# Batches two to four of a linear-attention and mixture-of-experts kernel: query features stream past stationary key sums, and denominators come out on the other 64 partitions

## The chip, the core and the metric

One core of a Trainium2 chip runs the whole program. The metric is the device time of one execution in microseconds (us); lower is better. The engines named below are PE (TensorE matmul; PEld is its weight load), DVE (VectorE), ACT (ScalarE), POOL (GpSimd) and SP (SyncE, which issues most DMAs). Each engine works through its own instruction list in the order in which the program writes it.

## The reference

Random-feature attention over 4 batches, 8 heads, 576 positions and 64 dimensions, with 128 features, and then a dense mixture of 4 experts on the 2304 tokens.

```python
def phi(x):                       # x scaled by 64 ** -0.25
    h = einsum('bhsd,md->bhsm', x, omega) - sum(x * x, -1, keepdims=True) / 2
    return exp(h - max(h, -1, keepdims=True)) / sqrt(m)
kv  = einsum('bhsm,bhsd->bhmd', k_p, v)
z   = sum(k_p, axis=2)
num = einsum('bhsm,bhmd->bhsd', q_p, kv)
den = einsum('bhsm,bhm->bhs', q_p, z)[..., None] + 1e-06
x   = (num / den), heads side by side: [2304, 512]
p   = domain_probs / (sum(domain_probs, -1) + 1e-09)
out = sum over e of p[:, e:e+1] * (relu(x @ w1[e]) @ w2[e])   # w1[e] is 512 x 1024
```

## The kernel before

**Experts.** The hidden width of each of the 4 experts is halved, so there are 8 (expert, half) visits for each of 4 token ranges ("u"): 0 to 511, 512 to 1023, 1024 to 1535 and 1536 to 2303. The token-range loop is the outer one. A visit works on blocks of 512 tokens (a few of 256): four *hidden steps* (`hidden`, lines 386 to 394, one of the half's four column groups each, called H0 to H3 below) and then one *output step* for every 128 tokens (`outputs`, lines 402 to 420, called O0 to O3). Numbers are held as two fp32r parts, high and low, and three products (high by high, high by low, low by high) stand for one f32 product. A hidden step on 512 tokens is 12 matmuls of 512 columns; an output step is 12 of 512 columns too. A hidden step ends with `relu` (ACT writes `hh`, then DVE writes `hl`) and, as a rule, one `split_w` (ACT writes a weight's high part, POOL its low part, and SP issues the load of a later weight). An output step ends with an accumulation on DVE (line 418) and one `split_w`. The second argument of the experts' matmuls is read from two rings of 1536 tokens, `x_hi` and `x_lo`.

**Attention.** A `Pair` is two heads of one batch. Batch 0 is done by `Pair`: four pairs in `begin`, before the experts start, and the rest of its queries in `first_rest` during the first visits. Batches 1, 2 and 3 are done by `Halves`, four pairs each, in `later_ticks`: a generator that yields between small parts, called ticks here. For one pair the ticks are, in order:

1. `project` (matmuls of keys and queries with omega into six PSUM banks), maxima of the keys
2. bias and exponentials of keys, first half
3. exponentials of keys, second half
4. the tails (the last 64 positions of both heads)
5. exponentials of queries, first head
6. exponentials of queries, second head; `sum_keys` (matmuls that add up `kv` and the sums `z`); loads of the next pair
7. `turn`: PE transposes of the query features into PSUM, copied to SBUF by DVE as `qt` (first head, and the tails)
8. `turn` of the second head
9. `numerators(0)` (first 256 positions)
10. `numerators(1)` (other 320 positions), `finish(0)`
11. `finish(1)`

In `numerators` the turned query features are the stationary operand and `kvs` (65 columns a head: 64 values and the sum) streams; the result has positions on partitions, so `finish` transposes it again on PE (lines 188 and 190), ACT writes `x_hi` from PSUM and DVE `x_lo`.

**Order.** The program order is written out by hand and kept: each engine executes in the order of emission. `emit` (line 605) walks through the visits; after each step it adds the step's share (1 for a step of 512 columns, 0.5 for a hidden step of 256) to a count and lets the ticks catch up to it. A batch has 48 ticks (4 to load and square the first pair, then 11 for each of 4 pairs), spread evenly over 0.9 of the batch's steps: 1.333 ticks a step for batch 1 (it has only 5 visits, numbers 3 to 7), 0.702 for batch 2 (visits 8 to 15), 0.833 for batch 3 (visits 16 to 23). So in batch 1 two neighbouring ticks now and then stand in one step, with no expert matmul between them; in batches 2 and 3 one or two steps lie between neighbouring ticks.

**PSUM.** All banks come from one pool of 8, handed out in turn by `bank`: the ninth request waits until the first bank has been read for the last time.

## Time and profile before

| | us |
|---|---|
| median of 3 runs | 975.51 (974.34 to 976.88) |
| the profiled execution | 980.6 |
| its span, first to last instruction | 978.2 |
| mean granted TensorE clock, share of full speed | 0.99 |
| PE busy | 957.4 (98%) |
| DVE busy | 369.2 (38%) |
| ACT busy | 342.2 (35%) |
| POOL busy | 371.8 (38%) |

The busy time of PE is made of records whose ends are modelled and overlap, so the pace of matmuls is read from start to start. Times within the trace count from the start of the span.

### The profile page before, as it was taken

Reading aid. Unit: us, or ns where it says so; the run is one execution under the profiler, and the core shown is the slowest. Engines: PE = TensorE matmul, PEld = TensorE weight load, DVE = VectorE, ACT = ScalarE, POOL = GpSimd, SP = SyncE. Lnnn points to the kernel's source line nnn. Section 1 sums busy time; section 2 is a strip of 40 time slices with the busy share of each in tenths; the row PEclk is TensorE's granted clock in tenths of the full one; section 3 lists DMA queues with packets and bytes.
Section 4 is the critical chain, followed back from the end, with each engine's and each line's share of the span. In section 5 each row is a group of like instructions: output and inputs, shape, how many; then the busy total and the mean of one; then the engine's idle time right before and its main releaser. Section 6 shows DMA issues by size and latency. Waiting matters only on the chain.

```text
span 978.2 us, 13669 instructions
## 1 busy us (share of the span) xinstructions
PE 957.4 (98%) x5216; PEld 808.6 (83%) x5216; DVE 369.2 (38%) x760; ACT 342.2 (35%) x806; POOL 371.8 (38%) x312
## 2 busy tenths in 40 slices
PE   6989999999999999999999999999999999999998
PEld 6978888887888888878888888888888888888887
DVE  3434445553334444343333354544311222222222
ACT  3345344433262324334326252434323221322120
POOL 3756543343342234444444344444414422431230
PEclk9799999999999999999999999999999999999999
DMA  6434544232432412423263342422313211221211
GB/s 152 108 107 119 171 126 135 78 111 80 126 89 80 141 48 86 145 69 90 82 202 99 112 135 76 135 78 75 109 63 86 76 34 64 87 65 31 78 33 65
DMA packets 60737, 94.09 MB, mean 96 GB/s; under 512 B 10176, under 2 KB 18560, under 8 KB 60672
## 3 DMA queue, kind: packets, MB, share of 16 engines
q1 hardware_dynamic: 60432, 92.92, 32.4%
q8 instruction: 41, 0.67, 0.3%
q10 hardware_dynamic: 240, 0.30, 0.1%
q14 instruction: 24, 0.20, 0.1%
HBM read 88.48 MB, written 4.72 MB: 95 GB/s over the span
## 4 chain that ended last, share of the span: by engine, by line
PE 94%; ACT 2%; DMA 1%; DVE 1%; POOL 1%; SPq 1%; issue 0%; POOLq 0%; ACTq 0%
PE g L392 14%; PE g L394 14%; PE g L393 14%; PE g L409 13%; PE g L411 13%; PE g L410 13%; PE kv L142 3%; PE nd L166 2%; PE qt_ps L151 2%; PE k_ps L234 1%; PE q_ps L234 1%; PE x_ps L188 1%; PE t_ps L238 1%; DMA k<-in_kT 1%; DMA va<-in_vn 1%; PE k_ps L114 1%
## 5 line engine op out<-in xcount | busy, mean ns | idle before, releaser
L378 POOL TENSOR_TENSOR w1l<-wraw,w1h 128x512 fp32r<-128x512 f32 x128 | 164.5, 1286 | 383.5 <-ACT w1h L375 374.9
L392 PE MATMUL g<-x_hi,w1h 128*128 128x512 f32 (+1 forms) x688 | 252.8, 367 | 0.0
L394 PE MATMUL g<-x_hi,w1l 128*128 128x512 f32 (+1 forms) x688 | 248.0, 360 | 0.0
L393 PE MATMUL g<-x_lo,w1h 128*128 128x512 f32 (+1 forms) x688 | 247.9, 360 | 0.0
L399 DVE SCALAR_TENSOR_TENSOR hl<-g,hh 128x512 fp32r<-128x512 f32 (+1 forms) x172 | 104.1, 605 | 345.4 <-ACT hh L398 345.4
L409 PE MATMUL g<-w2h,hh 128*128 128x512 f32 x576 | 228.4, 397 | 0.2 <-ACT hh L398 0.2
L411 PE MATMUL g<-w2h,hl 128*128 128x512 f32 x576 | 225.5, 391 | 0.0
L410 PE MATMUL g<-w2l,hh 128*128 128x512 f32 x576 | 225.0, 391 | 0.0
L398 ACT ACTIVATE hh<-g 128x512 fp32r<-128x512 f32 (+1 forms) x172 | 91.0, 529 | 375.0 <-PE g L394 374.8
L378 POOL TENSOR_TENSOR w2l<-wraw,w2h 128x512 fp32r<-128x512 f32 x128 | 163.1, 1289 | 144.0 <-ACT w2h L375 143.4
L418 DVE SCALAR_TENSOR_TENSOR acc<-g,pr,acc 128x512 f32<-128x512 f32 x126 | 94.6, 750 | 192.9 <-PE g L411 192.5
L394 PEld LDWEIGHTS g<-x_hi,w1l 128*128 128x128 f32 x688 | 131.0, 190 | 21.0
L392 PEld LDWEIGHTS g<-x_hi,w1h 128*128 128x128 f32 x688 | 131.1, 190 | 20.7 <-issue 0.5
L393 PEld LDWEIGHTS g<-x_lo,w1h 128*128 128x128 f32 x688 | 131.1, 190 | 19.5
L411 PEld LDWEIGHTS g<-w2h,hl 128*128 128x128 f32 x576 | 108.2, 188 | 24.1 <-DVE hl L399 1.1
L409 PEld LDWEIGHTS g<-w2h,hh 128*128 128x128 f32 x576 | 108.4, 188 | 23.5 <-ACT hh L398 0.7
L410 PEld LDWEIGHTS g<-w2l,hh 128*128 128x128 f32 x576 | 108.3, 188 | 21.3
L375 ACT ACTIVATE w2h<-wraw 128x512 fp32r<-128x512 f32 x124 | 76.2, 635 | 104.2 <-PE g L411 55.1
L375 ACT ACTIVATE w1h<-wraw 128x512 fp32r<-128x512 f32 x124 | 77.8, 627 | 0.1
L265 ACT ACTIVATE kp<-k_ps,nbk 128x128 f32<-128x128 f32 x96 | 27.4, 379 | 34.1 <-DVE nbk L259 34.1
L166 PEld LDWEIGHTS nd<-kvs,qt 128*128 128x128 f32 x256 | 33.9, 196 | 3.5 <-DVE qt L157 1.5
L166 PE MATMUL nd<-kvs,qt 128*128 128x65 f32 x256 | 33.0, 273 | 1.4 <-DVE qt L157 1.4
(82 smaller groups left out, 599.4 us busy)
## 6 DMA issues: line engine op xcount, KB each, us to landing
wraw<-in_w SPq DMA_DIRECT2D x256, 256.0 KB, 2.7
out<-acc SPq DMA_DIRECT2D x18, 256.0 KB, 3.2
va<-in_vn SPq DMA_DIRECT2D x16, 256.0 KB, 5.5
k<-in_kd SPq DMA_DIRECT2D x12, 288.0 KB, 3.1
q<-in_qd SPq DMA_DIRECT2D x12, 288.0 KB, 4.6
k<-in_kn SPq DMA_DIRECT2D x12, 288.0 KB, 4.9
q<-in_qn SPq DMA_DIRECT2D x12, 288.0 KB, 5.2
q<-in_qT SPq DMA_DIRECT2D x4, 160.0 KB, 3.4
```

The source lines that it names most:

```text
L166: nc.tensor.matmul(nd[:, t, cs], self.query_tile(j, 2 * part + t), self.kv[:, cs], start=True, stop=True)
L375: hi.activation(a, t, AF.Copy)
L378: lo.tensor_tensor(c, t, f32(a), ALU.subtract)
L392: nc.tensor.matmul(ps[:, :n], wa[:, w], x_hi[:, k, cs], start=(k == 0), stop=False)
L393: nc.tensor.matmul(ps[:, :n], wa[:, w], x_lo[:, k, cs], start=False, stop=False)
L394: nc.tensor.matmul(ps[:, :n], wc[:, w], x_hi[:, k, cs], start=False, stop=(k == KC - 1))
L398: nc.scalar.activation(ha, ps[:, :n], AF.Relu)
L399: nc.vector.scalar_tensor_tensor(hc, ps[:, :n], 0.0, f32(ha), ALU.max, ALU.subtract)
L409: nc.tensor.matmul(ps, ha[:, ts_], wa, start=(c == 0), stop=False)
L410: nc.tensor.matmul(ps, ha[:, ts_], wc, start=False, stop=False)
L411: nc.tensor.matmul(ps, hc[:, ts_], wa, start=False, stop=(c == FH - 1))
L418: nc.vector.scalar_tensor_tensor(acc[i], ps, sc, acc[i], ALU.mult, ALU.add)
```

## The change

For batches 1 to 3 (`Halves`) the layouts and four methods change:

- **Key sums.** The value tiles `va` and `vb` hold, for each pair, 64 columns of ones, the second head's values, the first head's values and 64 columns of ones (`VZ` = 256 columns instead of 130). `sum_keys` streams 128 columns a head instead of 65 (256 instead of 130 for the tails), so the sum `z` comes out 64 times, once for each column of ones. The result is split into high and low fp32r parts, `kvh` by ACT and `kvl` by DVE.
- **Turn.** `turn(part)` takes a part of the positions of both heads instead of one head. ACT writes a high part `qth`, DVE a low part `qtl`.
- **Numerators.** The key sums are the stationary operand and the turned queries stream, in three fp32r products a head: 6 matmuls of 256 or 320 columns. The result has dimensions on partitions: 64 partitions hold the numerators of a head and the other 64 its denominator, repeated. ACT copies the denominators, plus 1e-6, to the numerators' partitions (`dn`).
- **Finish.** DVE takes the reciprocal of `dn` (128 x 256 or 128 x 320 elements) and multiplies with each head's numerators in PSUM, ACT writes `x_hi` and POOL `x_lo`. There are no transposes in it.
- **Ticks.** Seven to eleven become: `turn(0)`; `numerators(0)`; `finish(0)` and then `turn(1)`; `numerators(1)`; `finish(1)`. The number of ticks and their pace stay.

Batch 0 keeps its way, on the new column order; its multiplication by the reciprocals is two instructions instead of one. The numbers of buffers change: `vb` 2 to 1, `kp` and `qp` 4 to 3, `xt` 2 to 1, `hh` and `hl` 6 to 5; the rings have a pool of their own.

```diff
     VW = P + 2
+    VZ = 2 * P
     WQ = 5 * P
...
     moe = ctx.enter_context(tc.tile_pool(name="moe", bufs=1))
+    xs = ctx.enter_context(tc.tile_pool(name="xs", bufs=1))
     psum = ctx.enter_context(tc.tile_pool(name="psum", bufs=8, space=bass.MemoryType.PSUM))
+    x_hi = xs.tile([P, NP, RING], F32R, name="x_hi")
+    x_lo = xs.tile([P, NP, RING], F32R, name="x_lo")
...
     prs = const.tile([P, NT // P], F32, name="prs")
-    vas = [const.tile([P, 4, VW], F32, name=f"va{i}") for i in range(2)]
-    vbs = [const.tile([P, NP, VW], F32, name=f"vb{i}") for i in range(2)]
-    x_hi = const.tile([P, NP, RING], F32R, name="x_hi")
-    x_lo = const.tile([P, NP, RING], F32R, name="x_lo")
+    vas = [const.tile([P, 4, VZ], F32, name=f"va{i}") for i in range(2)]
+    vbs = [const.tile([P, NP, VZ], F32, name=f"vb{i}") for i in range(1)]
...
+    OWN = [slice(D + 1, 2 * D + 2), slice(0, D + 1)]
...
             self.b, self.hp = b, hp
-            self.va, self.vb = vas[hp % 2], vbs[b % 2]
+            self.va, self.vb = vas[hp % 2], vbs[0]
             self.kp = {}
...
             cols = slice(self.hp * P, (self.hp + 1) * P)
-            eng.dma_start(self.va[:, :, 1:P + 1], vn[self.b, :512, cols].rearrange("(t p) c -> p t c", p=P))
+            eng.dma_start(self.va[:, :, D:D + P], vn[self.b, :512, cols].rearrange("(t p) c -> p t c", p=P))
...
             rows = vn[self.b, 512:].rearrange("p (h j d) -> p h j d", j=2, d=D)
-            eng.dma_start(self.vb[:D, :, 1:D + 1], rows[:, :, 0])
-            eng.dma_start(self.vb[D:, :, D + 1:P + 1], rows[:, :, 1])
+            eng.dma_start(self.vb[:D, :, P:P + D], rows[:, :, 1])
+            eng.dma_start(self.vb[D:, :, D:P], rows[:, :, 0])
...
             size = "t" if n == 1 else ""
-            f = att.tile([P, n, M], F32, tag=which + "p" + size, name=which + "p", bufs=2 if n == 1 else 4)
+            f = att.tile([P, n, M], F32, tag=which + "p" + size, name=which + "p", bufs=2 if n == 1 else 3)
             for i in range(n):
...
             kv = bank("kv")[:, :VW]
-            nc.tensor.matmul(kv, self.kp[2][:, 0], self.vb[:, self.hp], start=True, stop=False)
+            cut = slice(D - 1, D - 1 + VW)
+            nc.tensor.matmul(kv, self.kp[2][:, 0], self.vb[:, self.hp, cut], start=True, stop=False)
             for j in range(2):
-                cs = slice(j * (D + 1), (j + 1) * (D + 1))
                 for t in range(4):
-                    nc.tensor.matmul(kv[:, cs], self.key_tile(j, t), self.va[:, t, cs], start=False, stop=(j == 1 and t == 3))
+                    nc.tensor.matmul(
+                        kv[:, OWN[j]], self.key_tile(j, t), self.va[:, t, cut][:, OWN[j]], start=False, stop=(j == 1 and t == 3)
+                    )
             self.kv = att.tile([P, VW], F32, tag="kvs", name="kvs", bufs=5)
...
                 for j in range(2):
-                    cs = slice(j * (D + 1), (j + 1) * (D + 1))
-                    nc.tensor.matmul(nd[:, t, cs], self.query_tile(j, 2 * part + t), self.kv[:, cs], start=True, stop=True)
+                    nc.tensor.matmul(nd[:, t, OWN[j]], self.query_tile(j, 2 * part + t), self.kv[:, OWN[j]], start=True, stop=True)
             if part:
...
             nc.vector.reciprocal(r, r)
-            xt = att.tile([P, 3, P], F32, tag="xt", name="xt")
-            nc.vector.tensor_tensor(
-                xt[:, :2].rearrange("p t (j d) -> p t j d", j=2), nd[:, :2, 1:P + 1].rearrange("p t (j d) -> p t j d", j=2),
-                r[:, :2, :, None].to_broadcast([P, 2, 2, D]), ALU.mult,
-            )
-            for j in range(2 * part):
-                own = slice(j * D, (j + 1) * D)
-                nc.vector.tensor_tensor(
-                    xt[:D, 2, own], nd[own, 2, 1 + j * D:1 + (j + 1) * D], r[own, 2, j:j + 1].to_broadcast([D, D]), ALU.mult
-                )
+            xt = att.tile([P, 3, P], F32, tag="xt", name="xt", bufs=1)
+            for j in range(2):
+                own, src = slice(j * D, (j + 1) * D), slice(1 + (1 - j) * D, 1 + (2 - j) * D)
+                nc.vector.tensor_tensor(xt[:, :2, own], nd[:, :2, src], r[:, :2, 1 - j:2 - j].to_broadcast([P, 2, D]), ALU.mult)
+                if part:
+                    nc.vector.tensor_tensor(xt[:D, 2, own], nd[own, 2, src], r[own, 2, 1 - j:2 - j].to_broadcast([D, D]), ALU.mult)
             self.num[part] = xt
...
             ps, nb = getattr(self, which + "_ps")[j], getattr(self, "nb" + which)
-            f = att.tile([P, 4, M], F32, tag=which + "p", name=which + "p", bufs=4)
+            f = att.tile([P, 4, M], F32, tag=which + "p", name=which + "p", bufs=3)
             for i in range(4):
...
-        def key_tile(self, j, t):
-            return self.kp[j][:, t]
-        def query_tile(self, j, t):
-            return self.qx[j][:, t]
+        def sum_keys(self):
+            kv = bank("kv")[:, :VZ]
+            nc.tensor.matmul(kv, self.kp[2][:, 0], self.vb[:, self.hp], start=True, stop=False)
+            for j in range(2):
+                cs = slice((1 - j) * P, (2 - j) * P)
+                for t in range(4):
+                    nc.tensor.matmul(kv[:, cs], self.kp[j][:, t], self.va[:, t, cs], start=False, stop=(j == 1 and t == 3))
+            self.kv_h, self.kv_l = (att.tile([P, VZ], F32R, tag=x, name=x) for x in ("kvh", "kvl"))
+            nc.scalar.activation(self.kv_h, kv, AF.Copy, scale=1.0 / M)
+            nc.vector.scalar_tensor_tensor(self.kv_l, kv, 1.0 / M, f32(self.kv_h), ALU.mult, ALU.subtract)
+        def turn(self, part):
+            n = 2 * P + part * D
+            self.qt_h, self.qt_l = (
+                att.tile([P, 2, n], F32R, tag=f"{x}1" if part else "qt", name=x, bufs=2 - part) for x in ("qth", "qtl")
+            )
+            ps = bank("qt_ps")
+            for j in range(2):
+                for t in range(2):
+                    nc.tensor.transpose(ps[:, (2 * j + t) * P:(2 * j + t + 1) * P], self.qx[j][:, 2 * part + t], ident)
+            pieces = [(ps.rearrange("p (j t) -> p j t", j=2), slice(0, 2 * P))]
+            if part:
+                pt = bank("qt_ps")[:, :P]
+                nc.tensor.transpose(pt, self.qx[2][:, 0], ident)
+                pieces.append((pt.rearrange("p (j t) -> p j t", j=2), slice(2 * P, n)))
+            for src, cs in pieces:
+                nc.scalar.activation(self.qt_h[:, :, cs], src, AF.Copy)
+                nc.vector.tensor_tensor(self.qt_l[:, :, cs], src, f32(self.qt_h[:, :, cs]), ALU.subtract)
+        def numerators(self, part):
+            n = 2 * P + part * D
+            if part:
+                ps = [bank("nd")[:, :n] for _ in range(2)]
+            else:
+                both = bank("nd")
+                ps = [both[:, j * n:(j + 1) * n] for j in range(2)]
+            dn = att.tile([P, n], F32, tag=f"dn{part}", name="dn", bufs=1)
+            for j in range(2):
+                w = slice((1 - j) * P, (2 - j) * P)
+                nc.tensor.matmul(ps[j], self.kv_h[:, w], self.qt_h[:, j], start=True, stop=False)
+                nc.tensor.matmul(ps[j], self.kv_l[:, w], self.qt_h[:, j], start=False, stop=False)
+                nc.tensor.matmul(ps[j], self.kv_h[:, w], self.qt_l[:, j], start=False, stop=True)
+            for j in range(2):
+                own, other = slice(j * D, (j + 1) * D), slice((1 - j) * D, (2 - j) * D)
+                nc.scalar.activation(dn[own], ps[j][other], AF.Copy, bias=EPS)
+            self.num[part] = ps, dn, n
+        def finish(self, part):
+            ps, dn, n = self.num.pop(part)
+            nc.vector.reciprocal(dn, dn)
+            for j in range(2):
+                own = slice(j * D, (j + 1) * D)
+                nc.vector.tensor_tensor(dn[own], ps[j][own], dn[own], ALU.mult)
+            t0 = self.b * S + 2 * P * part
+            cut = min(n, -t0 % RING or n)
+            for a, m in ((0, cut), (cut, n - cut)):
+                if m:
+                    c = (t0 + a) % RING
+                    hi, lo = (x[:, self.hp, c:c + m] for x in (x_hi, x_lo))
+                    nc.scalar.activation(hi, dn[:, a:a + m], AF.Copy)
+                    nc.gpsimd.tensor_tensor(lo, dn[:, a:a + m], f32(hi), ALU.subtract)
...
             yield
-            p.turn(0, nc.vector)
-            p.turn(2, nc.vector)
-            yield
-            p.turn(1, nc.vector)
+            p.turn(0)
             yield
             p.numerators(0)
+            yield
+            p.finish(0)
+            p.turn(1)
             if hp + 1 < NP:
...
             p.numerators(1)
-            p.finish(0)
             if hp + 1 < NP:
...
-    W1B, W2B, RAWB, HB, AB = 6, 6, 4, 6, 7
+    W1B, W2B, RAWB, HB, AB = 6, 6, 4, 5, 7
     W = {}
...
         make_identity(nc, ident)
-        for t in vas[:1]:
-            nc.gpsimd.memset(t[:, :, 0:VW:VW - 1], 1.0)
-        for t in vbs[:1]:
+        def ones_a(t):
+            t = t.rearrange("p t (i d) -> p t i d", d=D)
+            nc.gpsimd.memset(t[:, :, 0], 1.0)
+            nc.gpsimd.memset(t[:, :, 3], 1.0)
+        def ones_b(t):
             nc.gpsimd.memset(t, 0.0)
-            nc.gpsimd.memset(t[:D, :, 0:1], 1.0)
-            nc.gpsimd.memset(t[D:, :, VW - 1:VW], 1.0)
+            nc.gpsimd.memset(t[:D, :, P + D:], 1.0)
+            nc.gpsimd.memset(t[D:, :, :D], 1.0)
+        ones_a(vas[0])
+        ones_b(vbs[0])
         ps[0].load_tails()
...
         ps[1].square("k", nc.gpsimd, rest)
-        nc.gpsimd.memset(vas[1][:, :, 0:VW:VW - 1], 1.0)
+        ones_a(vas[1])
         keys(0)
...
         ps[3].square("k", nc.gpsimd, rest)
-        nc.gpsimd.memset(vbs[1], 0.0)
-        nc.gpsimd.memset(vbs[1][:D, :, 0:1], 1.0)
-        nc.gpsimd.memset(vbs[1][D:, :, VW - 1:VW], 1.0)
...
         "qn": rows(q[1:]),
-        "vn": v.transpose(0, 2, 1, 3).reshape(B, S, H * D),
+        "vn": v.reshape(B, H // 2, 2, S, D)[:, :, ::-1].transpose(0, 3, 1, 2, 4).reshape(B, S, H * D),
         "omT": inputs["omega"].T,
...
```

## Rows read from the trace of the kernel before

**Rows 1.** The page: busy time, share of the span and instructions of each engine.
```profile
PE 957.4 (98%) x5216; PEld 808.6 (83%) x5216; DVE 369.2 (38%) x760; ACT 342.2 (35%) x806; POOL 371.8 (38%) x312
```

**Rows 2.** The timeline of PE in batch 2: start us, length us, engine, line, what. The first and the last of 18 expert matmuls of 256 columns in a row, then of 21 of 512 columns.
```profile
290.64 0.28 PE L392 MATMUL g<-x_hi,w1h 128*128 128x256 f32 x1
...
292.64 0.28 PE L394 MATMUL g<-x_hi,w1l 128*128 128x256 f32 x1
...
299.93 0.40 PE L392 MATMUL g<-x_hi,w1h 128*128 128x512 f32 x1
...
304.62 0.39 PE L394 MATMUL g<-x_hi,w1l 128*128 128x512 f32 x1
```

**Rows 3.** The chain that ended last, in order of time, in the same stretch: start us, us taken on the chain, what. The tails' matmul of `sum_keys` for the first pair of batch 2, its `numerators(0)`, its `numerators(1)` and the transposes of `finish(0)`. An f32 matmul is two instructions.
```profile
288.08 0.22 PE kv L138 x2
...
305.01 0.84 PE nd L166 x8
...
308.70 0.84 PE nd L166 x8
309.54 0.28 PE nd L168 x2
309.81 0.22 PE x_ps L188 x2
```

**Rows 4.** The timeline of PE: the first transposes of `finish(1)` of that pair, and the expert matmul that follows its last.
```profile
312.68 0.38 PE L188 MATMUL x_ps<-ident,xt 128*128 128x128 f32 x2
...
313.19 0.50 PE L409 MATMUL g<-w2h,hh 128*128 128x512 f32 x1
```

**Rows 5.** The timeline of PE in batch 0, f32 matmuls that stream 128 columns, and what follows them.
```profile
10.60 2.17 PE L114 MATMUL k_ps<-om,k 128*128 128x128 f32 x18
...
12.61 0.39 PE L138 MATMUL kv<-vb,kp 128*128 128x130 f32 x2
```

**Rows 6.** Groups of instructions on DVE, shapes apart: line, engine, operation, out and in, shapes, count, then busy us and mean ns of one.
```profile
L399 DVE SCALAR_TENSOR_TENSOR hl<-g,hh 128x512 fp32r<-128x512 f32 x116 | 80.3, 692 | 273.2 <-ACT hh L398 273.2
...
L199 DVE TENSOR_TENSOR x_lo<-x_ps,x_hi 128x256 fp32r<-128x256 f32 x16 | 6.8, 425 | 8.3 <-ACT x_hi L198 8.0
...
L171 DVE RECIPROCAL r<-r 128x4 f32<-128x4 f32 x16 | 2.8, 178 | 0.5
...
L66 DVE RECIPROCAL prs<-prs 128x18 f32<-128x18 f32 x1 | 0.3, 267 | 0.0
```

**Rows 7.** The same view of ACT.
```profile
L398 ACT ACTIVATE hh<-g 128x512 fp32r<-128x512 f32 x116 | 69.4, 598 | 251.9 <-PE g L394 251.8
...
L198 ACT ACTIVATE x_hi<-x_ps 128x256 fp32r<-128x256 f32 x16 | 6.3, 391 | 27.6 <-PE x_ps L188 27.6
...
L198 ACT ACTIVATE x_hi<-x_ps 128x128 fp32r<-128x128 f32 x4 | 1.1, 270 | 2.1 <-PE x_ps L190 2.1
```

**Rows 8.** Timelines of PE, ACT and DVE about two ticks of the first pair of batch 2. First a tick behind a hidden step (its PE work starts at 308.54), then one behind an output step (its PE work starts at 295.49).
```profile
308.54 1.00 PE L166 MATMUL nd<-kvs,qt 128*128 128x65 f32 x8
...
309.23 0.62 ACT L375 ACTIVATE w1h<-wraw 128x512 fp32r<-128x512 f32 x1
...
309.97 0.16 DVE L170 TENSOR_SCALAR r<-nd 128x6 f32<-128x6 f32 x1
...
295.49 0.71 PE L151 MATMUL qt_ps<-ident,qp 128*128 128x128 f32 x5
295.95 0.48 PE L409 MATMUL g<-w2h,hh 128*128 128x512 f32 x1
...
296.36 0.88 DVE L157 COPY qt<-qt_ps 128x512 f32<-128x512 f32 x2
```

**Rows 9.** The timeline of PE at a place of batch 1 where a turn and the numerators that read it stand in one step, and a row of the waits of PE on DVE over the whole run (us in total, times, longest us).
```profile
229.75 0.88 PE L166 MATMUL nd<-kvs,qt 128*128 128x65 f32 x6 [1.40 <-DVE qt L157]
...
PE x_ps L188 <- DVE xt L173: 1.8, 2, 0.9
```

**Rows 10.** Busy time by stretch of 1 us: the stretch, its length, busy us (instructions) of PE, PEld, DVE, ACT and POOL, the granted TensorE clock as a share of 2.4 GHz, DMA share, GB/s.
```profile
38.00:39.00 1.00, 0.00 (x0) 0.00 (x0) 0.00 (x0) 1.00 (x6) 1.00 (x2) 1.00 0.00 0
...
41.00:42.00 1.00, 1.00 (x6) 1.00 (x7) 0.93 (x4) 0.12 (x1) 1.00 (x2) 0.50 0.00 0
47.00:48.00 1.00, 1.00 (x9) 1.00 (x8) 0.00 (x0) 0.26 (x1) 0.42 (x1) 0.72 0.43 162
...
66.00:67.00 1.00, 0.00 (x0) 0.00 (x0) 0.00 (x0) 1.00 (x3) 0.46 (x1) 1.00 0.76 244
...
71.00:72.00 1.00, 1.00 (x9) 1.00 (x9) 0.00 (x0) 0.29 (x2) 0.38 (x1) 0.78 0.00 0
...
230.00:231.00 1.00, 1.00 (x9) 0.91 (x9) 0.30 (x2) 0.00 (x0) 0.23 (x1) 1.00 0.00 0
```

**Rows 11.** The start: the timeline of POOL and of SP's queue.
```profile
0.99 0.20 POOL masks.py:197 MEMSET ident<- 128x128 f32 x1
...
8.53 0.11 POOL L465 MEMSET va<- 128x8 f32 x1 [6.96 <-DMA va<-in_vn]
8.56 0.53 POOL L467 MEMSET vb<- 128x520 f32 x1
9.12 0.58 SPq L98 DMA_DIRECT2D vb<-in_vn  x1
...
18.13 2.69 POOL L106 TENSOR_TENSOR k<-k 64x512 f32<-64x512 f32 x2 [4.36 <-DMA k<-in_kT]
```

## The prediction

> **What bounds the kernel now.** I read the page's busy times first: PE is busy in 98% of the span and no other engine in more than 38% [rows 1]. So a microsecond that PE does not need is a microsecond won, and one that PE waits is lost; the other engines matter where PE waits for them. Then the timeline of PE for its pace from start to start: 18 expert matmuls of 256 columns follow each other in 2.00 us, 0.118 us each, and 21 of 512 columns at 4.69 / 20 = 0.2345 us [rows 2]. A step of 12 matmuls of 512 columns thus takes 2.8 us. Then the chain that ended last, for what attention costs on PE [rows 3], and the timelines of PE, ACT and DVE about single ticks, for what stands in each queue there [rows 8].
>
> **What PE gains.** For a pair of `Halves`, `numerators(0)` takes 0.84 us, `numerators(1)` 0.84 + 0.28 and the transposes of `finish(0)` 0.22 [rows 3]; those of `finish(1)` take 313.19 - 312.68 = 0.51 [rows 4]. Together 2.69 us go. Twelve products come: six of 256 columns at 0.118 and six of 320 at 0.118 + 64 x (0.2345 - 0.118) / 256 = 0.147, together 1.59 us.
>
> The key sums grow. The 16 instructions of 128 instead of 65 columns: 128 columns ran at (12.61 - 10.60) / 18 = 0.112 us [rows 5], 65 at 0.84 / 8 = 0.105 [rows 3], so +0.11 a pair. The tails go from 130 to 256 columns, which no row shows. Their two instructions take 0.22 now [rows 3], as two of 65 or of 128 columns nearly do; if what sets this is the weights' load, nothing is added, if it is the columns, 0.22 x 256 / 130 = 0.43, so +0.21. I take the second. The Trainium skill (FP8 and Floating Point Precision, TensorE Precision Notes) says that true FP32 passes four times through the array; 4 x 256 columns at 2.4 GHz would be an estimated 0.43 us, and 4 x 130 would be 0.22, as the row has it. By that the sum stays as it is; by the weights' load it would be 2.5 us lower.
>
> Net for a pair: 1.59 + 0.32 - 2.69 = -0.78 us; for 12 pairs **-9.4** (-13 if neither key sum grows). The turn's nine transposes stay. Two waits of batch 1 go too, because what they wait for is gone or moved: 1.4 us of numerators on the turn's copy, and 0.9 of `finish`'s transposes on DVE (the other 0.9 of that row is batch 0's) [rows 9]: **-2.3**.
>
> **What PE waits for now.** Each engine works in program order, so I follow one pair's queues from a tick that holds `finish(0)` and `turn(1)`. Let T be the start of its PE work.
>
> Behind a hidden step, ACT is free at T + 1.3 (the weight's split, 309.23 + 0.62 against 308.54) and DVE at T + 1.43 (309.97) [rows 8]. Then:
> - DVE: the reciprocal of 128 x 256. Rows show 0.178 us for 4 elements and 0.267 for 18 [rows 6]: (0.267 - 0.178) / 14 = 6.4 ns an element on 0.153 fixed. For 256 that is 1.78 us, for 320 2.18. It ends at T + 3.2. This is the largest unknown. From below, DVE's other work grows by (692 - 425) / 256 = 1.04 ns an element [rows 6], which gives 0.42 and 0.49 us. I take the slope of the operation itself, from two rows of it, and keep the other.
> - DVE: two multiplications with PSUM, 0.43 each [rows 6], overlapping a little: T + 4.0.
> - ACT: `x_hi`, which waits for them, 0.39 [rows 7]: T + 4.4. Queued behind it on ACT, since `finish(0)` is written ahead of `turn(1)`: `qth`, 512 columns and then 128, 0.60 and 0.27 [rows 7]: T + 5.25.
> - DVE: `qtl`, 0.69 and some 0.29: T + 5.9.
>
> The Trainium skill (VectorE: DVE Perf Modes, First, the fixed hardware budget) says that the reciprocal is an iterated divide with a repeat count of 8. At that page's 0.96 GHz eight cycles would be an estimated 8.3 ns an element against the 6.4 of the rows, some 0.5 us more at 256 elements, and the sum would be about 6 us higher; the rows decide.
>
> PE meanwhile does five transposes (0.46 to the next start [rows 8], some 0.6 with what follows) and the next step, and comes to `numerators(1)` at T + 3.4 if that stands one step later. It waits 1.85 us for `qth`, does two products, and waits 0.35 for `qtl`: 2.2 us. Behind an output step DVE is free at T + 0.87 [rows 8], so all is 0.56 earlier: 1.7 us. With two steps between, PE comes at T + 6.2 and waits for nothing.
>
> Laying the 48 ticks of a batch on its steps by the pacing rule gives the 12 pairs:
> - one step between, hidden: pairs 1, 2, 3 of batch 1 (counting from 0), pair 0 of batch 2, pair 1 of batch 3: 5 x 2.2 = 11.0
> - one step between, output: pairs 2, 3 of batch 2 and 0, 3 of batch 3: 4 x 1.7 = 6.8
> - two between: pair 1 of batch 2, pair 2 of batch 3: 0
> - none between: pair 0 of batch 1, 5.25 - 0.6 + 0.35 = 5.0
>
> `turn(0)` and `numerators(0)` stand in one step in pair 2 of batch 1 (ACT split to T + 1.3, `qth` to 1.9, `qtl` to 2.6, PE there at 0.5, less 0.25 of products): 1.9. With a step between they cost nothing, since PE comes at T + 3.3.
>
> The banks: the two of `numerators(1)` are read until `finish(1)` has multiplied, T + 1.43 + 2.18 + 0.49 = T + 4.1 for the first. `project` takes six banks. In pair 2 of batch 1 `finish(1)` and the next `project` stand in one step, and the ninth request after the first of those banks is the second query bank, wanted at T + 1.15: 2.95 us. In two more pairs (0 of batch 1, 2 of batch 3) one step lies between: some 0.55 each. Together 4.1.
>
> Sum of the waits: 11.0 + 6.8 + 5.0 + 1.9 + 4.1 = **+28.8**.
>
> **The clock.** After a whole us of idle PE at 38 the granted clock was at the 1.2 GHz level (0.50) by 41 and came back in the stretch at 47; after the idle at 66 it was back in the stretch at 71; after a wait of 1.4 us that ended at 229.75 it stayed at 1.00 [rows 9, 10]. So a fall costs up to half of some 6 us, 3 us, or in the shorter case under 2; I take 1.5. Of the new waits, the two near 3 us and longer get it, and half of the nine of 1.4 to 1.9: 2 x 1.5 + 4.5 x 1.5 = **+9.5** (0 to 33).
>
> **The rest.** In the start POOL sets ones and zeros ahead of the tails' load: (0.53 - 0.20) / 392 = 0.84 ns an element, so 0.96 + 2 x 0.31 instead of 0.11 + 0.53 [rows 11], and SP, which waits there with every later load queued behind, starts them 0.9 us later; the squares at 18.13, which PE awaits, wait for one of these loads. With the split multiplication of batch 0: **+1.0**. The memset of the second `vb` that goes is POOL's later in the start. Fewer buffers cost nothing that I can find: a block uses four `hh`, and the fifth is asked for a whole step before the next is; the third `kp` or `qp` is a pair ahead. POOL's `x_lo` is read a token range later. DVE's and ACT's added work (some 3 us each for a pair) lies beside PE's steps except where counted.
>
> **Sum.** -9.4 - 2.3 + 28.8 + 9.5 + 1.0 = +27.6. On the profiled execution 980.6 + 27.6 = 1008.2; the median of the runs stands 5.1 below that execution, so 975.5 + 27.6 = 1003.
>
> **Rivals.**
> 1. *The reciprocal costs as other DVE work does* (0.42 and 0.49 us). Then behind a hidden step the wait is 0.85, behind an output step 0.36, with no step between 3.65, the bank costs 1.3 once: 5 x 0.85 + 4 x 0.36 + 3.65 + 1.9 + 1.3 = 12.5, one fall of the clock 1.5, the sum +3.3 and the time 979, or 975 with the larger gain on PE. Not slower, then. It decides where the reciprocal takes under about 0.4 us. Against it: two rows of the same operation, one slope; for it, that the longest seen is 18 elements.
> 2. *Every new wait drops the clock for six us*: 11 x 3 = 33 instead of 9.5, 1027. For it: the idle us at 38. Against: the 1.4 us that did not.
> 3. *The waits without the clock*: 1003 - 9.5 = 994. This lies in the forecast's own range.
> 4. *The change hides its waits and gives its gain alone*: 975.5 - 9.4 - 2.3 + 1.0 = 965. It needs `qth` and `qtl` by T + 3.4, against a queue that ends at T + 5.9; nothing in the rows shortens that by 2.5 us.
>
> **Chances.** Forecast (with rival 3 in it, 990 to 1016) 0.68; rival 2 0.12; rival 1 0.13; rival 4 0.07. A measurement of this kernel tells about 0.3%, 3 us, from no change. Rival 1 splits over faster 0.03, same 0.09 and slower 0.01; rival 4 is faster. So faster 0.10, same 0.09, slower 0.81. The range goes from 975 to 1028; it leaves out rival 4, half of rival 1 and the top of rival 2, some 0.17.
>
> **What would show it.** Right: a reciprocal of 128 x 256 near 1.8 us; PE waits of about 2 us ahead of the `kvh`, `qth` products, put down to ACT `qth` and DVE `qtl`; `x_hi` on ACT waiting for DVE; one wait of `project` on DVE's multiplication; lower clock after some of these; products at 0.12 and 0.15 us. Wrong: a short reciprocal, or PE as dense in the stretches of batches 1 to 3 as now, with the span shorter by 0.8 us a pair.

## The result, and the profile after

The changed kernel takes 986.36 us (median of 4, 984.81 to 987.68) against 975.41 of before: a ratio of 1.0111, 95% interval 1.0091 to 1.0131. It is slower by 11.0 us. The forecast was 27.6 us slower, so the sign was right and the size two and a half times too large. The profiled execution takes 984.8 us with a span of 983.0. Of the executions below one, of the kernel with the turn first, took 2400.72 us; it is in that kernel's median (957.87 without it) and not in its ratio. Every ratio is to executions of before in its own session, whose medians lay between 975.33 and 976.07, so that differences between kernels of different sessions are good to about 1 us. (Lines of the changed kernel are not those of before: L333 is the reciprocal, L336 the multiplications, L343 `x_hi`, L309 `qth`, L310 `qtl`, L323 to L325 the three products of `numerators`, L453 to L455 a hidden step, L470 to L472 an output step, L527 to L533 the ones and zeros of the value tiles.)

The page of the changed kernel, busy times and the shares of the chain that ended last:

```profile
PE 942.4 (96%) x5084; PEld 795.6 (81%) x5084; DVE 410.6 (42%) x728; ACT 377.9 (38%) x890; POOL 392.2 (40%) x339
...
PE 88%; DVE 5%; ACT 2%; DMA 1%; POOL 1%; issue 1%; SPq 0%; ACTq 0%; DVEq 0%; POOLq 0%
```

Against [rows 1] PE does 15 us less, and still the time grows: PE waits. The waits of the changed kernel (us in total, times, longest us):

```profile
PE nd L323 <- ACT qth L309: 20.3, 11, 4.6
...
PE nd L325 <- DVE qtl L310: 1.6, 8, 0.2
PE g L470 <- DVE dn L336: 1.6, 1, 1.6
```

Eleven waits for `qth` make 20.3 us, where before had 1.4 and 0.9 us at this place [rows 9]. What lies behind one of them is in the timelines of the changed kernel at the first pair of batch 2, a tick behind a hidden step with T = 309.01:

```profile
309.01 0.60 PE L302 MATMUL qt_ps<-ident,qp 128*128 128x128 f32 x4
...
310.45 1.74 DVE L333 RECIPROCAL dn<-dn 128x256 f32<-128x256 f32 x1
...
313.54 0.42 ACT L343 ACTIVATE x_hi<-dn 128x256 fp32r<-128x256 f32 x1 [3.73 <-DVE dn L336]
313.86 0.75 ACT L309 ACTIVATE qth<-qt_ps 128x512 fp32r<-128x512 f32 x2
...
314.47 0.89 DVE L310 TENSOR_TENSOR qtl<-qt_ps,qth 128x512 fp32r<-128x512 f32 x2 [0.97 <-ACT qth L309]
...
314.66 0.41 PE L323 MATMUL nd<-qth,kvh 128*128 128x320 f32 x1 [2.19 <-ACT qth L309]
...
315.41 0.62 PE L325 MATMUL nd<-qtl,kvh 128*128 128x320 f32 x1 [0.20 <-DVE qtl L310]
```

ACT stands idle for 3.73 us because `x_hi`, first in its queue, waits for DVE's reciprocal and multiplications; `qth`, whose input PE had finished by 309.7, comes only then, and PE has waited 2.19 us; at the four other places behind a hidden step it waits 1.83 to 1.90. The reciprocal in the groups of DVE:

```profile
L333 DVE RECIPROCAL dn<-dn 128x320 f32<-128x320 f32 x12 | 25.7, 2143 | 0.3 <-ACT dn L328 0.3
...
L333 DVE RECIPROCAL dn<-dn 128x256 f32<-128x256 f32 x12 | 20.9, 1743 | 0.6 <-ACT dn L328 0.6
```

1.74 and 2.14 us, against 1.78 and 2.18 from the slope of [rows 6]. From these two, (2143 - 1743) / 64 = 6.25 ns an element. The Trainium skill's repeat count of 8 (VectorE: DVE Perf Modes, First, the fixed hardware budget), read as eight cycles an element at that page's 0.96 GHz, gives an estimated 8.3 ns; the measured 6.25 are six such cycles, so the count is not the rate seen here.

The granted clock behind that wait (same columns as [rows 10]):

```profile
313.00:314.00 1.00, 0.00 (x0) 0.00 (x0) 0.49 (x2) 0.47 (x2) 0.00 (x0) 1.00 0.03 8
...
316.00:317.00 1.00, 1.00 (x5) 0.96 (x4) 0.65 (x1) 0.56 (x2) 1.00 (x1) 0.50 0.00 0
```

It fell to the 1.2 GHz level for 3.4 us. From batch 1 on there are five such stretches, where the profiles of before have none; by half their length they cost some 8.5 us.

Two things in the trace the forecast has not. The first is the pace of a hidden step:

```profile
303.56 0.39 PE L453 MATMUL g<-x_hi,w1h 128*128 128x512 f32 x1
...
308.77 0.40 PE L455 MATMUL g<-x_hi,w1l 128*128 128x512 f32 x1
```

These are the first and the last of 24 matmuls in a row: 5.21 / 23 = 0.2265 us from start to start, where [rows 2] have 0.2345. The matmuls are the same. The second is the start, POOL and SP's queue:

```profile
1.51 0.31 POOL L527 MEMSET va<- 128x256 f32 x1
...
2.01 0.95 POOL L531 MEMSET vb<- 128x1024 f32 x1
...
3.97 0.57 SPq L103 DMA_DIRECT2D vb<-in_vn  x1
```

POOL sets the ones at 1.51 us without waiting, and SP issues the tails' load at 3.97, where before had 9.12 [rows 11].

Stage by stage, from the start of the first keys' projection of batches 1, 2 and 3 in the timelines of PE (us; the kernels below are those of the experiments):

| kernel | up to batch 1 | batch 1 | batch 2 | from batch 3 on | span |
|---|---|---|---|---|---|
| before | 112.4 | 153.5 | 243.0 | 469.3 | 978.2 |
| before, second profile | 108.2 | 153.6 | 243.0 | 469.3 | 974.1 |
| changed | 103.0 | 166.9 | 244.8 | 468.4 | 983.0 |
| before, rings last | 107.2 | 152.9 | 240.8 | 464.9 | 965.8 |
| before, ones first | 103.5 | 155.3 | 243.0 | 469.3 | 971.2 |
| before, both of these | 105.2 | 152.8 | 240.8 | 464.8 | 963.6 |
| changed, reciprocal early | 103.4 | 159.1 | 237.5 | 462.1 | 962.1 |
| changed, turn first | 104.1 | 155.5 | 236.5 | 460.7 | 956.8 |
| changed, both of these | 103.4 | 151.2 | 236.4 | 460.7 | 951.7 |

### The profile page after: what moved, and what is told of

It reads as the page before. It is cut to its first block, busy times and chain, and to the rows that moved or that the text cites. A ratio compares the mean times of both kernels' runs of the same rounds, so it can differ in the third digit from the quotient of the medians.

```text
span 983.0 us, 13493 instructions
## 1 busy us (share of the span) xinstructions
PE 942.4 (96%) x5084; PEld 795.6 (81%) x5084; DVE 410.6 (42%) x728; ACT 377.9 (38%) x890; POOL 392.2 (40%) x339
## 4 chain that ended last, share of the span: by engine, by line
PE 88%; DVE 5%; ACT 2%; DMA 1%; POOL 1%; issue 1%; SPq 0%; ACTq 0%; DVEq 0%; POOLq 0%
PE g L453 13%; PE g L455 13%; PE g L454 13%; PE g L470 13%; PE g L472 13%; PE g L471 13%; PE kv L288 2%; DVE dn L333 2%; PE k_ps L236 1%; PE nd L325 1%; PE q_ps L236 1%; DVE dn L336 1%; PE qt_ps L302 1%; DVE qtl L310 1%; POOL w1l L439 1%
## 5 line engine op out<-in xcount | busy, mean ns | idle before, releaser
L453 PE MATMUL g<-x_hi,w1h 128*128 128x512 f32 (+1 forms) x688 | 250.1, 363 | 0.0
L455 PE MATMUL g<-x_hi,w1l 128*128 128x512 f32 (+1 forms) x688 | 246.4, 358 | 0.0
L470 PE MATMUL g<-w2h,hh 128*128 128x512 f32 x576 | 227.5, 395 | 2.1 <-DVE dn L336 1.6
L472 PE MATMUL g<-w2h,hl 128*128 128x512 f32 x576 | 225.1, 391 | 0.0
L453 PEld LDWEIGHTS g<-x_hi,w1h 128*128 128x128 f32 x688 | 132.4, 192 | 18.3 <-issue 0.7
L455 PEld LDWEIGHTS g<-x_hi,w1l 128*128 128x128 f32 x688 | 131.8, 192 | 19.1
L470 PEld LDWEIGHTS g<-w2h,hh 128*128 128x128 f32 x576 | 108.5, 188 | 25.2 <-issue 2.5
L472 PEld LDWEIGHTS g<-w2h,hl 128*128 128x128 f32 x576 | 108.3, 188 | 24.4 <-DVE hl L460 1.3
L344 POOL TENSOR_TENSOR x_lo<-dn,x_hi 128x256 fp32r<-128x256 f32 (+3 forms) x28 | 19.8, 713 | 70.9 <-ACT x_hi L343 66.3
L333 DVE RECIPROCAL dn<-dn 128x256 f32<-128x256 f32 (+1 forms) x24 | 46.6, 1943 | 0.9 <-ACT dn L328 0.9
L343 ACT ACTIVATE x_hi<-dn 128x256 fp32r<-128x256 f32 (+3 forms) x28 | 11.0, 407 | 76.8 <-DVE dn L336 76.8
```

What stands on the lines that cost most here:

```text
L333: nc.vector.reciprocal(dn, dn)
L453: nc.tensor.matmul(ps[:, :n], wa[:, w], x_hi[:, k, cs], start=(k == 0), stop=False)
L455: nc.tensor.matmul(ps[:, :n], wc[:, w], x_hi[:, k, cs], start=False, stop=(k == KC - 1))
L470: nc.tensor.matmul(ps, ha[:, ts_], wa, start=(c == 0), stop=False)
L472: nc.tensor.matmul(ps, hc[:, ts_], wa, start=False, stop=(c == FH - 1))
```

## The experiments

**Before, a second profile.** No edit.

> The kernel before, unchanged, for a second profile. Theory: the profiled execution of before that the prediction rests on (980.6 us) is a slow one within this kernel's own spread, and what differs is the start: there PE idled 3.5 us near 16 and then ran at the 1.2 GHz level until 30 and again from 41 to 47. Then this profile shows batch 1's first projection earlier than 112.45 us and a span nearer to 973. Rival: the profile only adds a constant; then the first projection stands at 112.45 again.

Measured: 975.37 us, as before; this profile's span is 974.1 and its first projection stands at 108.2 us. All later stages agree with the first profile to about 0.1 us. So 4 of the 9.4 us by which the changed kernel's start leads in the two traces were that one execution's slow start. Times of the start are read with this in mind.

**Before, rings in the last pool.**

```diff
+    xs = ctx.enter_context(tc.tile_pool(name="xs", bufs=1))
...
+    x_hi = xs.tile([P, NP, RING], F32R, name="x_hi")
+    x_lo = xs.tile([P, NP, RING], F32R, name="x_lo")
...
-    x_hi = const.tile([P, NP, RING], F32R, name="x_hi")
-    x_lo = const.tile([P, NP, RING], F32R, name="x_lo")
```

> The kernel before, with only the two rings moved into a pool of their own behind all other pools, as the change does. In the changed kernel's trace the hidden steps' matmuls of 512 columns follow each other every 0.227 to 0.229 us instead of 0.234, also after 700 us, where no attention is left. Theory: this comes from where the rings lie; 1392 such matmuls by 6.5 ns less, some 9 us: 966. Rival: it comes from what attention no longer does, or from the five hh buffers; then this kernel is as before, 975.

Measured: 966.83 us, ratio 0.9913 (0.9899 to 0.9927): 8.5 us for an edit that moves two tiles. The groups of PE, here and in the second profile of before:

```profile
L393 PE MATMUL g<-x_hi,w1h 128*128 128x512 f32 x464 | 185.0, 399 | 0.0
```

```profile
L392 PE MATMUL g<-x_hi,w1h 128*128 128x512 f32 x464 | 187.8, 405 | 0.0
```

6 ns less for each matmul of 512 columns; from start to start 0.2266 against 0.2342 us (mean over the stretch from 700 to 930 us, where no attention is left). Over the whole run, with the steps beside attention, the means are 0.2309 and 0.2370: 1392 of these by 6 ns are 8.4 us. Those of 256 columns go from 0.1187 to 0.1198, 672 of them by 1 ns, which takes 0.7 back. The stages from batch 1 on are 7.3 us shorter than in the second profile of before, so the theory of the place holds; why the place matters is the next question.

**Why the place matters.** The addresses of the tiles are read from the compiled program. In before the rings start at 26752 bytes of each partition and the weights at 134112: remainders modulo 2048 of 128 and 992, a difference of 864. In the last pool, rings and weights share a remainder (992 and 992; in the changed kernel 608 and 608), because all tiles of the pool ahead of the rings, the weights' among them, are 2048 bytes long. Four paddings tell the remainder from the region.

```diff
+    pad = const.tile([P, 8], F32, name="pad")
+    nc.gpsimd.memset(pad, 0.0)
     x_hi = const.tile([P, NP, RING], F32R, name="x_hi")
```

> The kernel before with 32 bytes of padding ahead of the rings, so that their start address is 32 more and everything behind them 32 more too. If the faster pace comes from the address modulo 64 (0 in before, 32 in the changed kernel), the hidden steps run at 0.227 us here and the time is some 966. If it comes from the region or the order of the pools, the pace stays 0.234 and the time 975.

Measured: 975.19 us, pace 0.2342. Rings and weights both move by 32 bytes, their difference stays, nothing changes.

```diff
     x_lo = const.tile([P, NP, RING], F32R, name="x_lo")
+    pad = const.tile([P, 296], F32, name="pad")
+    nc.gpsimd.memset(pad[:, :8], 0.0)
```

> The kernel before with 1184 bytes of padding behind the rings. The rings stay where they were; the weights, hh, hl and all else behind them move up by 1184 bytes. In before the rings start 128 bytes above a multiple of 2048 and the weights 992 above one; with the rings in the last pool both have the same remainder, and the hidden steps are faster. Theory of remainders: here both have 128, the hidden steps' matmuls of 512 columns come every 0.227 us and the time is some 967. Theory of the region or the order of the pools: the pace stays 0.234, the time 975.

Measured: 967.31 us, ratio 0.9920 (0.9905 to 0.9935), pace 0.2266. The rings did not move; the weights now have the rings' remainder.

```diff
+    pad = xs.tile([P, 296], F32, name="pad")
+    nc.gpsimd.memset(pad[:, :8], 0.0)
     x_hi = xs.tile([P, NP, RING], F32R, name="x_hi")
```

> The kernel before with the rings in a pool behind all others and 1184 bytes of padding ahead of them in that pool, so that the rings lie in the faster region but with the remainder 128 modulo 2048 against 992 of the weights, as in before. Theory of remainders: 0.234 us a matmul and 975. Theory of the region or the order: 0.227 and 967.

Measured: 975.99 us, ratio 1.0014 (0.9995 to 1.0033), pace 0.2341. The region is the changed kernel's, the gain is gone. The groups of PE with the padding behind the rings, and with the padding in the last pool:

```profile
L394 PE MATMUL g<-x_hi,w1h 128*128 128x512 f32 x464 | 185.3, 399 | 0.0
```

```profile
L395 PE MATMUL g<-x_hi,w1h 128*128 128x512 f32 x464 | 187.8, 405 | 0.0
```

```diff
     x_lo = const.tile([P, NP, RING], F32R, name="x_lo")
+    pad = const.tile([P, 8], F32, name="pad")
+    nc.gpsimd.memset(pad, 0.0)
```

> The kernel before with 32 bytes of padding behind the rings. Rings and weights then have the same remainder modulo 64 (both 0; in before 0 and 32), but not modulo 128 or more (rings 0, weights 0 modulo 128 as well; 128 and 1024 modulo 2048, so different from 256 up). If the same remainder modulo 64 or 128 is enough, the pace is 0.227 us and the time 967. If the whole 2048 counts, 0.234 and 975.

Measured: 973.78 us, ratio 0.9974 (0.9962 to 0.9986), pace 0.2333. The difference is now 896; the same remainder modulo 64 and 128 is not enough and gives 1 of the 7 ns. So a hidden step's matmuls follow each other faster where rings and weights start at the same remainder, whichever it is (992, 608 and 128 were tried), than where they start 864 or 896 bytes apart modulo 2048.

The two operands of one matmul agree less far than the tiles' starts: the rings' slice of a block of 512 tokens starts at a multiple of 2048 bytes within the tile, and the weights' slice `wa[:, w]` at k x 512 bytes for the k-th of four partial sums. With the rings last, the matmuls of all four k keep the same pace, 0.2262 to 0.2270 us between 700 and 930 us. What counts is therefore the address modulo 512 at most, and by the last padding more than modulo 128; 256 or 512 stays open, and so does what in the chip makes it so. The output steps fit this: their operands `hh` and `w2h` lie in one pool in every kernel, and their pace is 0.2270 to 0.2276 in all of them. The timeline of PE in before, first and last of 12 matmuls of an output step in a row, 2.50 / 11 = 0.2273 us:

```profile
292.75 0.39 PE L409 MATMUL g<-w2h,hh 128*128 128x512 f32 x1
...
295.25 0.40 PE L411 MATMUL g<-w2h,hl 128*128 128x512 f32 x1
```

**Before, ones set first.**

```diff
+        nc.gpsimd.memset(om[D:], -QS * QS / 2)
+        for t in vas:
+            nc.gpsimd.memset(t[:, :, 0:VW:VW - 1], 1.0)
         ps[0].load("k", [first, rest])
...
-        nc.gpsimd.memset(om[D:], -QS * QS / 2)
...
         ps[0].load_v()
         make_identity(nc, ident)
-        for t in vas[:1]:
-            nc.gpsimd.memset(t[:, :, 0:VW:VW - 1], 1.0)
...
-        nc.gpsimd.memset(vas[1][:, :, 0:VW:VW - 1], 1.0)
```

The fill of `om` moves up with the ones; it stays POOL's first work of the program.

> The kernel before, with only the ones of the two value tiles set by POOL ahead of the first loads instead of behind the load of the values. In before, POOL waits 6.96 us for that load and SP's next loads wait for POOL; in the changed kernel POOL sets its ones at 1.5 us without a wait, and batch 1's first projection starts 9.4 us earlier than in before's trace. Theory: that wait is the cause; then the tails' loads are issued near 4 us, PE has no idle stretch near 16 and batch 1's first projection stands near 103 to 107: 967 to 971. Rival: the start's gain is chance of the clock or of the loads; then 975.

Measured: 973.01 us, ratio 0.9972 (0.9961 to 0.9983). The timeline of POOL and SP's queue in this kernel:

```profile
1.59 0.53 POOL L467 MEMSET vb<- 128x520 f32 x1
...
3.98 0.57 SPq L98 DMA_DIRECT2D vb<-in_vn  x1
```

The wait is gone and the tails' load goes out 5.1 us earlier. The first projection stands at 103.5, as in the changed kernel; but the time is only 2.3 us less, below the 4 to 8 expected. Batch 1 took 1.7 us longer in this profile, where the clock fell once, behind the wait of 1.4 us that left it at 1.00 in before. The wait for the values' load was the cause, and what it is worth is smaller: 2.3 us alone, and 966.83 - 965.53 = 1.3 us on top of the rings (below).

**Before, with both side gains and its own attention.** The edits of the rings and of the ones together.

> The kernel before with both side gains, the rings in a pool behind the others and the ones set ahead of the loads, and its own attention. If the two gains add up: 975 less 9 and less 5 to 9, 957 to 961. The changed kernel stands against this one as its attention alone: 986 against some 959, so the new attention as written costs 27 us, about the sum of the prediction without its start. Rival: the gains do not add, and the new attention costs 15 or less.

Measured: 965.53 us, ratio 0.9901 (0.9884 to 0.9917). The gains fall short of the 957 to 961 expected: together they are 9.9 us. The changed kernel is 986.36 - 965.53 = 20.8 us slower than this one, and this difference is the new attention, with the fewer buffers and batch 0's split multiplication in it, which were not tried apart. The forecast for the attention alone was -9.4 - 2.3 + 28.8 + 9.5 = +26.6.

**Changed, turn ahead of finish.**

```diff
-            p.finish(0)
-            p.turn(1)
+            p.turn(1)
+            p.finish(0)
```

> The changed kernel, with turn(1) written ahead of finish(0) in their common tick. Theory of the prediction: PE's 20 us of waiting for qth are the reciprocal's time on DVE seen through ACT's order (x_hi ahead of qth). Then qth and qtl are ready at T + 2.2 and T + 2.9, before PE comes at T + 3.4; the waits fall from some 24 us to some 6 (the pair with no step between, turn(0) with numerators(0), the banks), the falls of the clock behind them go: 986 less 18 to 25, 961 to 968. Rival: the reciprocal's 1.74 us on DVE holds up hl and acc in any order, and the wait moves to the expert steps; then 980 or more.

Measured: 958.25 us, ratio to before 0.9822 (0.9805 to 0.9838); 28.1 us less than the changed kernel from two lines swapped, and below the 961 to 968 expected. The profile is of a second run:

> The changed kernel with turn(1) ahead of finish(0), once more, for a profile of it: its runs took 958 us. Theory: PE's waits for qth are left only where the turn and the numerators stand in one step, 4 us instead of 20, and qtl's near none; the granted clock stays at 1.00 after batch 0. Rival: qth's waits are as before and the time was won by something else.

Measured: 958.59 us. Its waits of PE, and the stretch from batch 1's second pair on:

```profile
PE nd L323 <- ACT qth L309: 2.6, 2, 1.4
PE t_ps L240 <- DVE dn L336: 2.3, 2, 1.8
PE g L470 <- DVE dn L336: 2.1, 1, 2.1
...
PE nd L325 <- DVE qtl L310: 0.4, 2, 0.2
```

```profile
140.00:700.00 560.00, 554.08 (x2966) 464.19 (x2965) 280.77 (x477) 249.59 (x594) 244.45 (x206) 1.00 0.35 107
```

Two waits for `qth` are left of eleven, 2.6 us of 20.3, and the granted clock is 1.00 throughout. The timelines of the same pair as above, batch 2's first:

```profile
299.45 0.76 ACT L309 ACTIVATE qth<-qt_ps 128x512 fp32r<-128x512 f32 x2
...
300.20 0.88 DVE L310 TENSOR_TENSOR qtl<-qt_ps,qth 128x512 fp32r<-128x512 f32 x2
...
300.99 1.74 DVE L333 RECIPROCAL dn<-dn 128x256 f32<-128x256 f32 x1
...
302.06 0.30 PE L323 MATMUL nd<-qth,kvh 128*128 128x320 f32 x1
...
302.94 0.39 PE L453 MATMUL g<-x_hi,w1h 128*128 128x512 f32 x1
```

`qth` and `qtl` are written before the reciprocal starts, and PE takes the products without a wait. The reciprocal still takes its time on DVE; nothing that PE needs stands behind it. The waits for `dn` (L336) are the banks that `project` or the next output step wants back.

**Changed, reciprocal a tick earlier.**

```diff
             for j in range(2):
                 own, other = slice(j * D, (j + 1) * D), slice((1 - j) * D, (2 - j) * D)
                 nc.scalar.activation(dn[own], ps[j][other], AF.Copy, bias=EPS)
+            nc.vector.reciprocal(dn, dn)
             self.num[part] = ps, dn, n
 
         def finish(self, part):
             ps, dn, n = self.num.pop(part)
-            nc.vector.reciprocal(dn, dn)
```

> The changed kernel, with the reciprocal moved from finish into numerators, one tick earlier; the order of finish(0) and turn(1) stays. Theory: behind a hidden step DVE then has only the two multiplications ahead of x_hi, qth is ready near T + 3.5 and qtl near T + 4.2: 0.1 to 0.8 us of wait for a pair instead of 2. Waits some 10 us, few falls of the clock: 968 to 974. It costs DVE a wait for dn in the numerators' tick. Rival: that wait holds up hl of the next step; then 980 or more.

Measured: 963.18 us, ratio to before 0.9867 (0.9853 to 0.9881), better than the 968 to 974 expected. The timelines of this kernel at the same pair:

```profile
297.14 1.75 DVE L329 RECIPROCAL dn<-dn 128x256 f32<-128x256 f32 x1 [0.76 <-ACT dn L328]
...
303.03 0.85 DVE L336 TENSOR_TENSOR dn<-nd,dn 64x256 f32<-64x256 f32 x2
303.91 0.42 ACT L343 ACTIVATE x_hi<-dn 128x256 fp32r<-128x256 f32 x1 [1.52 <-DVE dn L336]
...
305.79 0.42 PE L325 MATMUL nd<-qtl,kvh 128*128 128x320 f32 x1 [0.20 <-DVE qtl L310]
```

The reciprocal runs at 297, under PE's next steps; ACT waits 1.52 us instead of 3.73, and PE 0.20 for `qtl` and nothing for `qth`. Three waits for `qth`, 5.9 us together, and two falls of the clock are left, all in batch 1.

**Changed, both.**

> The changed kernel with both: turn(1) ahead of finish(0), and the reciprocal a tick earlier. Theory: little is left to wait for beside the two ticks that stand in one step: 958 to 965. Rival: no better than turn first alone.

Measured: 954.15 us, ratio to before 0.9777 (0.9764 to 0.9791), below the 958 to 965 expected. This is the best of all kernels here, 32.2 us below the changed kernel. What is left of the waits:

```profile
PE nd L323 <- ACT qth L309: 2.6, 2, 1.4
...
PE nd L325 <- DVE qtl L310: 0.6, 3, 0.2
PE g L470 <- ACT hh L459: 0.5, 1, 0.5
```

In this kernel the banks' waits are gone too. Against the kernel before with the same rings and start (965.53) the new attention wins 11.4 us once PE need not wait for it (in the profiles 1.7 of this stands in the start, which varies by as much between profiles).

## Why the prediction was right in its sign and wrong in its size

The step that failed is the one called the rest: it priced the fewer buffers at nothing, left the rings' own pool out, and put the start at +1.0 us. Measured, the rings' place and the start are worth -9.9 together (-8.5 for the rings; the start -1.3 behind them, -2.3 alone), 10.9 us from the forecast. Two terms of the attention were mis-sized as well, by some 1.5 and 3 us. Point by point:

- **What bounds the kernel: right.** PE's own work falls and the time rises by what PE waits.
- **PE's gain: mis-sized.** Forecast -0.78 us a pair. Batch 2 takes 236.4 us with the changed kernel's attention and little waiting (turn first and reciprocal early) and 240.8 with that of before on the same rings: -4.4 / 4 = -1.1 us a pair. From batch 3 on it is 460.7 against 464.8, -1.0 a pair. In batch 1, with the waits set apart (3.2 of 151.2 and 2.5 of 152.8), only -0.6 a pair. Together -10.8 us for the forecast -9.4. In batch 2 two terms went wrong. The 16 instructions of the key sums cost no more at 128 columns than at 65 (1.70 us from start to next start in both, priced at +0.11). And the experts' own matmuls, read from start to next start, take 0.3 us a pair less: the first one behind f32 work is slow (in before's timeline 296.27 - 295.95 = 0.32 us to the next start, where its neighbours have 0.23), and fewer of these returns are left, which I did not price. That the tails' 256 columns double (0.43 us) was right. Why batch 1 gains less is not settled. The old waits that go there are 2.5 us for the forecast 2.3.
- **The reciprocal: right,** 1.74 and 2.14 us for 1.78 and 2.18. Rival 1, a reciprocal as cheap as other DVE work, is excluded by this.
- **PE's waits: right in mechanism, place and nearly in size.** 20.3 + 1.6 + 1.6 = 23.5 us are seen for 28.8. Behind a hidden step 1.83 to 2.19 and 0.20 were measured for 1.85 and 0.35; behind an output step four waits of 1.19 to 1.20 for 1.29 (1.85 - 0.56); with no step between 4.65 for some 5.0; for `turn(0)` with `numerators(0)` in one step 1.26 and 0.23 for 1.9. The banks were the worst: 1.58 us once for 4.1, and it was an output step that waited, not `project`. The clock was nearly right: five falls of 3.4 us at half speed are some 8.5 us for 9.5. Both are better judged by taking them away: turn first gives back 28.1 us and the early reciprocal 4.1 more, 32.2 in all, and 3.2 us of waits remain there (2.6 + 0.6); together 35.4, for the forecast 38.3. The waits and falls that I add up from rows make 32. The rest is of the size of what a wait costs beside its own length. Behind an output step, where the clock stayed at 1.00, the timeline of PE in the changed kernel has

```profile
418.76 0.42 PE L323 MATMUL nd<-qth,kvh 128*128 128x320 f32 x1 [1.19 <-ACT qth L309]
...
420.21 0.40 PE L470 MATMUL g<-w2h,hh 128*128 128x512 f32 x1
```

  From the first of the six products to the matmul behind the last it is 1.45 us, 0.20 of it the wait for `qtl`, against 302.94 - 302.06 = 0.88 with the turn first: 0.37 us more, or by estimate some 4 us for the ten waits ahead of `numerators(1)`.
- **The start: wrong sign.** I saw POOL's wait for the values' load in [rows 11], priced the longer memsets behind it, and did not ask whether the wait would stay. In before the two columns of ones were set by one access that steps across the loaded columns; after, each memset sets a block of its own at either end of them, and POOL no longer waits. Setting the ones ahead of the load in before takes the same wait away and brings the first projection to the same place, so the wait was the cause; that the block form is what freed it was not tried by itself.
- **The rings: not priced at all.** "The rings have a pool of their own" was taken for bookkeeping. Nothing in the trace of before pointed at it, except that hidden steps ran at 0.2345 us and output steps, with as many matmuls of 512 columns, were not compared with them. In before's trace output steps run at 0.2273: two paces for the same work was the hint.

Taken together: +27.6, less 10.9 (rings and start, -9.9 for +1.0), 1.6 (PE's gain and the old waits, -13.3 for -11.7) and 2.9 (waits and clock, 35.4 for 38.3), is +12.2 for a measured +11.0. The 1.2 left is within what the start varies. The errors all lay on one side, and the largest had nothing to do with the attention. The range, 975 to 1028, held the time, but it had been drawn for the waits and the clock, not for the rings; of the rivals, none was the case.

## What to carry to other kernels

In a kernel bound by one engine, price a change by the queue in front of what that engine needs next, with every instruction written ahead of it: here two swapped lines were worth 28 us, most of eleven waits behind a 1.7 us reciprocal and the clock that fell five times behind them. Work whose result nobody needs soon goes behind work that is awaited, on every queue that both pass. And a change of layout or pools has a price of its own: compare the pace of equal instructions in different stages before and after, and run the move alone.

## What the runs showed of the hardware

Matmuls of 512 columns follow each other every 0.2266 us when the tiles that they stream and hold start at the same address modulo 2048 bytes (three remainders tried), every 0.2342 when these differ by 864 (three kernels), and every 0.2333 when they differ by 896; as the slices within the weights' tile lie 512 bytes apart and share the pace, what counts is the address modulo 512 at most. The reciprocal on DVE costs 6.25 ns an element of the row, six times the 1.04 ns that other DVE work costs [rows 6].

The length of PE's wait alone did not decide whether the granted clock fell. In the changed kernel, from batch 1 on, it fell in or right behind the wait of 4.65 us and behind four of the five of 1.83 to 2.19 us, and stayed at 1.00 behind the six of 1.19 to 1.58. With the turn first, waits of 1.81 and 2.09 us left it at 1.00; and the wait of 1.40 us in batch 1 left it there in before and was followed by a fall in the kernel with the ones first.
